# A gated long convolution beside a product-key expert layer on one core: residual taken from the normalized tokens by matrix products, stored tiles read back plainly, norm sums on ScalarE, wider table rows, and shifted priorities in the planner

## The chip, the cores and the metric

The kernel runs on one core of one Trainium2 chip. The metric is device time in microseconds (us) of one execution. Engines are called as the profile calls them: PE (matrix products; PEld is its weight load), DVE (VectorE), ACT (ScalarE), POOL (GpSimd, which here issues the gathers) and SP (the queue that issues all other transfers). All arithmetic is float32.

## The reference

2048 tokens of width 448 are normalized, and three things are added: the tokens themselves, a gated long convolution, and a product-key expert layer.

```python
xn = _layernorm(x, axis=-1)                 # x = A_q, 2048 x 448
return x + _A_ref(xn, ...) + _B_ref(xn, ...)

# _A_ref: four-tap causal filter on k, times v, then a causal convolution of length 2048 per channel
kv = k_shift * v
y = irfft(rfft(kv padded) * rfft(ssm_k padded))[:S] + kv * ssm_D
return q * y                                # q = xn

# _B_ref: 16 heads, two score rows of 64 keys each; the best 2 of each, the best 2 of the 4 sums
s1 = einsum("nhd,ed->nhe", q1, k1); s2 = einsum("nhd,ed->nhe", q2, k2)
g = softmax(top_s)                          # top_e: which 2 of 4096 experts, per head
act = gelu(einsum("nd,nhkd->nhk", xf, u[top_e]))
out = einsum("nhk,nhk,nhkd->nd", g, act, v[top_e])
```

Each token thus needs 32 rows of u and 32 rows of v. The kernel keeps u and v side by side in one table `uv`, 3584 bytes a row, and gathers 65,536 of them, 235 MB.

## The kernel before

**Tiles.** The tokens form 16 tiles T of 128. For the experts a tile is 8 batches, 128 batches in all (b = 8T + j). A batch is four gathers of 128 rows each (L536), which put one (token, expert) pair on each of 128 partitions, four times. The ring holds 5 batches, and at most 6 gathers are on their way.

**A batch** (`batch`, L560): DVE multiplies the gathered u rows with the tokens (L569, one instruction over 1792 elements); the tokens stand in PSUM, repeated by `spread` (L557), once for a tile. ACT sums each of the four products (L575) and applies gelu (L577). POOL, and DVE from batch 104 on (`LATE`), forms the coefficients (L583, L582). PE multiplies them with the v rows into the accumulator `pv` (L588). After the eighth batch `fold` (L599) ends the tile and `store` (L611) writes it from the tile `fo` to the output.

**Residual.** `fold` loads the tile of x again into `fo` (L603). For T below `T_OUT0` = 9, PE adds it to `pv` by a product with the identity (L605) and ACT copies `pv` to `fo` (L606); from T = 9 on, DVE adds `pv` to `fo` (L608).

**Scores.** In the beginning 16 blocks of weights are loaded (`weights`, L355), multiplied by the keys (L365), transposed and split into two parts. For each tile `turn` (L404) transposes the normalized tokens, `score` (L419) makes four blocks of 11 products (L427 to L431), DVE finds the best (L436, L443), and `pick` (L449) turns them into indices and weights.

**Convolution.** It is a Fourier transform in matrix products, over two groups of channels: part 0 (112 channels, while the scores still run) and part 1 (336 channels, after them, in the space that the score weights leave). Each part has three stages: in (`conv_in`, L628: L638 to L659), middle (33 frequencies, `spectrum` and `inverse`, L681 and L732, one 64 KB matrix loaded for each, L678) and out (`conv_out`, L777: transposes L789, copies L791, products L796, gates on DVE L807 and L812). The gate multiplies the convolution with the normalized tokens. For early tiles it does so in place in `XA` (L807), and needs nothing else of the normalized tokens afterwards; for later tiles it goes to another tile, `g0t` or `G` (L812).

**How the gated convolution reaches the output.** Tiles 0 to 13 (`T_OUT1` = 14) are stored before part 1 is done; when it is, POOL adds `XA` to the stored output by 14 accumulating transfers (L944). For tiles 9 to 15 ACT first copies `g0t` (and, for 14 and 15, `G`) into `XA` (L932), and tiles 14 and 15 add `XA` to `fo` on DVE (L951) before they are stored.

**Norm.** DVE makes mean and variance of a tile (L322, L323), a Newton iteration gives the inverse root (L326 to L337), ACT normalizes in place (L341). Tile 0 is done first, then 1 to 3, then 4 to 15 together.

**What sets the order.** Everything is handed as an operation to a planner (`Plan`, L92): engine, assumed duration, what it reads and writes, and a key. The planner simulates the engines in time and, whenever one is free, gives it the ready operation with the smallest key; the order that results is the program order on every engine, and nothing is reordered on the chip. The keys are due times, written by hand (`tb`, `due`, `CONV`, L209 to L213). The durations are constants, such as 1.0 us for the four products of a batch (L596) and 2.8 us for a block of scores (L432). Each gather also waits for one PE operation that lies before it in the plan (`LEAD`, L956 to L970).

At the end of the program a flag is read; a second pass for ties would run only if it is set, which it isn't here.

Of the kernel before, what the change touches and what calls it, by code (L numbers as in the profile page):

```python
# [34 lines left out]
T_OUT0, T_OUT1 = 9, 14  # L35


def tables():
# [37 lines left out]
    return cst1.astype(np.float32), cst2.astype(np.float32), fq.reshape(NQ, P, P).astype(np.float32)  # L76
# [7 lines left out]
class Op:  # L84
    __slots__ = ("eng", "dur", "fn", "deps", "users", "key", "acq", "rel", "nb", "start", "end", "name", "left", "avail", "pace", "last")
# [6 lines left out]
class Plan:  # L92
# [123 lines left out]
LEAD = 0.5  # L216
LATE = 104
# [16 lines left out]
def one_pass(ctx, tc, x, wq, kk, uv, kvh, cst1, cst2, fq, out, flag):  # L234
# [20 lines left out]
    nmr = ap.tile([P, NT], F32, name="nmr")  # L255
    nw = ap.tile([P, 64], F32, name="nw")
# [29 lines left out]
    def switch():  # L286
# [4 lines left out]
        x1[1] = view(sp.tile([P, 84 * XW], F32, name="x1b"), 1)  # L291
# [157 lines left out]
    def pick(T, b0, b1, key, two=1):  # L449
# [65 lines left out]
        op("ACT", 0.2 + 0.008 * n, lambda: put(idx, 0), r=["pl"], w=[("idx", t, i) for t in tiles for i in half], key=key, name="idx")  # L515
        op("ACT", 0.2 + 0.008 * n, lambda: put(gat, 1), r=["pl"], w=[("gat", t, i) for t in tiles for i in half], key=key, rel=("bank", s), name="gat")
# [43 lines left out]
    def batch(T, j):  # L560
# [36 lines left out]
    ob = [S1[:, 0:D], S1[:, D:2 * D]]  # L597

    def fold(T):  # L599
        k = tb(NB * T + NB) + 1.0  # L600
        o = fo[:, :]
        last = NB * T + NB - 1
        load(o, x[T], MB * D, ["fo"], k - 12.0, nb=k - 16.0, name="xr")  # L603
        if T < T_OUT0:
            op("PE", 0.85, lambda: nc.tensor.matmul(pv[:, :D], ident, o, start=False, stop=False), r=["fo", "c1", ("pv", 0)], w=[("pv", NB)], key=k - 2.0, name="res")  # L605
            op("ACT", act(D), lambda: last_val(nc.scalar.activation(o, pv[:, :D], AF.Copy).ins, last), r=[("pv", j) for j in range(NB + 1)], w=["fo", "pv"], key=k, name="fold")  # L606
# [57 lines left out]
    fmb = [S1[:, P * i:P * i + P] for i in range(4)]  # L664
# [10 lines left out]
    def matrix(q, k):  # L675
        u = nf[0] % 4
# [346 lines left out]
```

## Time and profile before

| | us |
|---|---|
| three runs | 940.2, 943.68, 949.0 (median 943.68) |
| the profiled execution | 950.11, span 948.3 |
| tile 0 stored (L612 issued) | 142.8 |
| scores of the last tile, part 0 of the convolution done | about 550 |
| middle of part 1 done, its out stage begins (first L789) | 829.6 |
| last gate of part 1 (L812) | 916.7 |
| last gather issued (L536) | 925.5 |
| last tile stored (L612 issued) | 940.2 |

The profiled execution is 0.7% above the median of the runs. A busy PE in such a page is not PE at its peak, since products are pipelined and the clock that PE is granted changes: 0.84 of full speed in the mean. Idle time of an engine is listed in the profile with what ended it; where two rows of PE and PEld name the same releaser and the same number of times, they are the same stop seen twice.

### The profile page before, as it was taken

To read this page: it belongs to the slowest core of one execution; us is meant where nothing else is said; L and a number is where in the kernel's file an instruction comes from. 1 tells how busy PE (TensorE), PEld (TensorE's weight loads), DVE (VectorE), ACT (ScalarE), POOL (GpSimd) and SP (SyncE) were. 2 spreads that over 40 slices of the span, in tenths; PEclk is the share of its full clock that TensorE was granted. 3 is DMA by queue.
4 is the path that set the end of the run, shared out by engine and by line. 5 is a ranking of instruction groups with operands and counts; after the bars stand their busy time and mean duration, and the time that the engine had idled before them with its cause. 6 is when DMAs were issued, how large, how long until landed. Compare 5 with 4: busy or idle time off the path is not lost.

```text
span 948.3 us, 13985 instructions
## 1 busy us (share of the span) xinstructions
PE 707.8 (75%) x4070; PEld 412.8 (44%) x4070; DVE 679.5 (72%) x1592; ACT 542.9 (57%) x1800; POOL 606.9 (64%) x754
## 2 busy tenths in 40 slices
PE   4777688677868898879888685666677988877671
PEld 2343455444535565546465453443333433344440
DVE  3479786788757887778777856777778999944451
ACT  2346275545554556656473475556577887855551
POOL 0036567688756765665657577787876776665564
PEclk9887779799878998889979778778789999987855
DMA  9998668788978887897779879999999899988898
GB/s 327 327 345 321 189 216 293 250 306 290 320 255 304 301 273 265 289 325 245 246 272 334 291 261 338 365 341 369 345 324 312 295 322 330 325 294 301 290 284 189
DMA packets 72214, 281.46 MB, mean 297 GB/s; under 512 B 10816, under 2 KB 35648, under 8 KB 72128
## 3 DMA queue, kind: packets, MB, share of 16 engines
q0 software_dynamic: 42976, 238.13, 73.5%
q1 hardware_dynamic: 29152, 42.35, 13.2%
q8 instruction: 34, 0.56, 0.2%
q14 instruction: 52, 0.43, 0.1%
HBM read 273.55 MB, written 6.88 MB: 296 GB/s over the span
## 4 chain that ended last, share of the span: by engine, by line
PE 29%; DVE 19%; issue 18%; POOL 12%; DMA 10%; ACT 7%; another core or an unknown queue 3%; SPq 0%; DVEq 0%; POOLq 0%; ACTq 0%
POOL ring L536 9%; DMA ring<-in_uv_dram,idx 8%; PE pv L588 5%; DVE SC L436 5%; DVE ring L569 5%; PE bank L655 4%; ACT ring L575 3%; PE bank L427 2%; PE bank L796 2%; DMA R<-in_wq_dram 2%; PE bank L428 2%; PE bank L429 2%; POOL cc L582 2%; DVE SC L443 2%
## 5 line engine op out<-in xcount | busy, mean ns | idle before, releaser
L536 POOL DMA_INDIRECT ring<-in_uv_dram,idx x512 | 506.9, 990 | 300.2 <-issue 95.4
L575 ACT ACTIVATE ring<-ring 128x448 f32<-128x448 f32 x512 | 288.5, 567 | 85.6 <-DVE ring L569 70.2
L569 DVE TENSOR_TENSOR ring<-ring,xs 128x1792 f32<-128x1792 f32 x128 | 257.4, 2016 | 95.6 <-DMA ring<-in_uv_dram,idx 81.5
L588 PE MATMUL pv<-ring,cc 128*32 128x448 f32 x1024 | 145.4, 650 | 69.8 <-POOL cc L582 34.4
L436 DVE MAX8 SC<-bank 128x8 f32<-128x64 f32 x512 | 118.5, 231 | 47.9 <-PE bank L431 21.7
L655 PE MATMUL bank<-c,S 128*64 128x132 f32 x896 | 77.5, 329 | 30.8 <-ACT ring L575 8.8
L427 PE MATMUL bank<-WR,xh 128*128 128x512 f32 x192 | 89.4, 466 | 10.9 <-DVE xl L416 4.9
L575 ACT ACTIVATION_READ_ACCUMULATOR ring<-ring 128x1 f32 x512 | 97.1, 190 | 0.0
L655 PEld LDWEIGHTS bank<-c,S 128*64 128x64 f32 x896 | 63.7, 165 | 65.3 <-ACT ring L575 24.4
L429 PE MATMUL bank<-WR,xl 128*128 128x512 f32 x192 | 82.7, 431 | 3.1 <-issue 2.5
L428 PE MATMUL bank<-WR,xh 128*128 128x512 f32 x192 | 82.8, 431 | 0.8 <-DVE WR L386 0.8
L588 PEld LDWEIGHTS pv<-ring,cc 128*32 128x32 f32 x1024 | 22.3, 116 | 122.6 <-POOL cc L582 46.0
L703 PE MATMUL bank<-x1b,S 128*128 128x336 f32 x132 | 51.6, 496 | 12.6 <-ACT x1b L767 5.0
L427 PEld LDWEIGHTS bank<-WR,xh 128*128 128x128 f32 x192 | 40.5, 211 | 42.0 <-issue 17.5
L659 ACT ACTIVATE x1b<-bank 128x264 f32<-128x264 f32 x84 | 30.8, 388 | 44.0 <-PE bank L655 32.5
L714 ACT ACTIVATE S<-bank 64x112 f32<-64x112 f32 x132 | 34.0, 257 | 37.1 <-PE bank L699 16.3
L443 DVE FIND_INDEX8 SC<-SC,bank 128x8 uint32<-128x256 f32 x128 | 52.7, 424 | 0.0
L720 DVE TENSOR_TENSOR S<-bank,S 128x224 f32<-128x224 f32 (+1 forms) x66 | 40.5, 618 | 13.8 <-issue 4.0
L582 POOL TENSOR_TENSOR cc<-sm,c 128x128 f32<-128x128 f32 x104 | 48.2, 463 | 3.3
L746 PE MATMUL bank<-S,c 128*128 128x112 f32 x264 | 42.0, 322 | 6.7 <-issue 2.7
L429 PEld LDWEIGHTS bank<-WR,xl 128*128 128x128 f32 x192 | 40.6, 211 | 14.3 <-issue 2.9
L365 PE MATMUL bank<-R 128*64 128x448 f32 x128 | 31.8, 631 | 19.7 <-DMA R<-in_wq_dram 15.6
(130 smaller groups left out, 1020.1 us busy)
## 6 DMA issues: line engine op xcount, KB each, us to landing
R<-in_wq_dram SPq DMA_DIRECT2D x16, 896.0 KB
S<-in_kvh_dram SPq DMA_DIRECT2D x28, 400.0 KB
ring<-in_uv_dram,idx POOLq DMA_INDIRECT x512
S<-in_fq_dram SPq DMA_DIRECT2D x66, 64.0 KB
fo<-in_x_dram SPq DMA_DIRECT2D x16, 224.0 KB
out_dram<-fo SPq DMA_DIRECT2D x16, 224.0 KB
out_dram<-XA POOLq DMA_DIRECT2D x14, 224.0 KB
XA<-in_x_dram SPq DMA_DIRECT2D x2, 1344.0 KB
```

The source lines that it names most:

```text
L427: nc.tensor.matmul(o, xh[:, c, :], wh[:, c, ns], start=(c == 0), stop=False)
L428: nc.tensor.matmul(o, xh[:, c, :], wl[:, c, ns], start=False, stop=False)
L429: nc.tensor.matmul(o, xl[:, c, :], wh[:, c, ns], start=False, stop=False)
L436: nc.vector.max(mx[:, 8 * n + j, :] if safe else m2[:, m, 2 * j:2 * j + 8], bank[s.i][:, 64 * j:64 * j + 64])
L443: nc.vector.max_index(m4i[:, 2 * m + g, :], m2[:, m, 8 * g:8 * g + 8], bank[s.i][:, 256 * g:256 * g + 256])
L536: g = nc.gpsimd.indirect_dma_start(dst, None, uv, bass.IndirectOffsetOnAxis(ap=idx[:, T % 8, r, j:j + 1], axis=0)).ins
L569: op("DVE", dve(m * D), lambda: nc.vector.tensor_mul(U[:, :m, :], U[:, :m, :], xs[:, :m, :D]), r=["xs"], w=u[:m], key=k, name="prod")
L575: op("ACT", 0.575, lambda r=r: nc.scalar.activation(U[:, r, :], U[:, r, :], AF.Copy, accum_out=aw[:, r:r + 1]), w=[u[r], ("aw", b % 4, r)] ...
L582: last_val(ve.tensor_mul(cc[b % 3], co[:, :, None].broadcast_to([P, 4, 32]), rep[:, None, :].broadcast_to([P, 4, 32])).ins, b - 3)
L588: v = nc.tensor.matmul(pv[32 * r:32 * r + 32, :D], cc[b % 3][:, r, :], ring[:, b % RING, r, D:], start=(j == 0), stop=(j == NB - 1), tile_ ...
L655: nc.tensor.matmul(o[64 * i:64 * i + 64, w * j:w * j + w], src, f1[:, i, :], start=True, stop=True, tile_position=(0, 64 * i))
L703: op("PE", 0.95 * n / 448 + 0.05, lambda t=t, sl=sl: nc.tensor.matmul(bank[sl.i][:, :n], fmb[u], x1[p][:, :, q, t, :], start=True, stop=True),
```

## The change

1. **Residual.** x is no longer loaded a second time. From the norm DVE makes dev = (variance + 1e-5) x rstd, the standard deviation (one more instruction in the Newton step). Once for a tile ACT makes `ds`, the identity times dev; PE adds ds times the normalized tile to `pv`, and for tiles from 9 (15) on the identity times `g0t` (`G`), in new functions `more` and `residual`. ACT ends every tile, with the mean as bias. L605, L608, L932 and L951 go.
2. **Stored tiles.** `T_OUT1` is 15. Instead of the accumulating transfers, SP loads the stored tiles 0 to 14 into the space of part 1's data (all columns for T below 9, the 336 of part 1 after), DVE adds `XA`, SP stores them again.
3. **Norm.** Tiles 4 to 15 get their sums from ACT: a copy with a running sum, a scaling, a square with a running sum.
4. **Tables.** The weights' rows are laid out as 7168 bytes for a partition instead of four of 1792; x lies by partitions, so that several tiles are one row; the frequency matrices are loaded in pairs, 34 loads instead of 66, into two buffers instead of four.
5. **Planner.** Operations get a group name, and `RANK` shifts the keys of each group by a line through four numbers over the range of the group's keys. Two orders are made explicit (`after=`): the copies L512 of one place, and the two gates of one chunk.

```diff
-T_OUT0, T_OUT1 = 9, 14
+T_OUT0, T_OUT1 = 9, 15
...
-    return cst1.astype(np.float32), cst2.astype(np.float32), fq.reshape(NQ, P, P).astype(np.float32)
+    turn = [i for ka in range(16) for i in (ka, 32 - ka)] + [16]
+    fq = fq.reshape(NQ, P, P)[turn].transpose(1, 0, 2).reshape(P, NQ * P)
+    return cst1.astype(np.float32), cst2.astype(np.float32), np.ascontiguousarray(fq.astype(np.float32))
...
 LEAD = 0.5
+RANK = {
+    "DMAc1": (25.0, 18.5, 21.0, 40.5), "DMAc2": (-8.5, -20.0, -9.5, -17.5), "DMAfb": (-29.5, 9.0, 67.0, 15.0),
...
+    "SPfb": (59.0, 65.5, 47.5, 62.5), "SPfm@sp0": (-32.0, -5.5, -8.0, -20.0), "SPfm@sp1": (9.0, 49.5, -6.0, 43.0), "SPkk": (4.0, -17.5, 2.0, 2.0),
...
+    "fin@out0": (-90.0, -32.0, -52.5, -95.0), "fin@out1": (-172.5, -183.0, -139.5, -189.5), "flag": (53.5, 83.5, 133.0, 121.0),
...
+    "pt": (-201.0, -329.0, -246.5, -149.0), "pw": (9.0, 9.0, 9.0, 0.0), "px": (2.0, -16.5, -10.5, -18.5), "res": (203.5, 163.5, 229.5, 139.0),
...
+    "res0": (-163.5, -58.5, -62.5, -78.0), "res1": (4.5, 80.5, 92.5, 108.5), "sc": (-60.5, -0.5, -0.5, -0.5), "spread": (53.5, -72.0, -207.0, -4.5),
...
+        ms = [(0.85, ds, slice(0, D), lambda: XA[:, T, :], ["ds", ("x", T)], "res"), (0.32, ident, slice(0, 112), lambda: g0t[:, T - T_OUT0, :], ["c1", ("G", 0)], "res0"),
...
-            op("PE", 0.85, lambda: nc.tensor.matmul(pv[:, :D], ident, o, start=False, stop=False), r=["fo", "c1", ("pv", 0)], w=[("pv", NB)], key=k - 2.0, name="res")
...
+        i = op("SP", 0.08, lambda T=T, c=c, w=w: nc.sync.dma_start(second["x1b"][:, w], out[T][:, c:]), r=["fb"], w=[("fb", T)], key=k, after=(stored[T],), name="SPfb")
...
     def load_x(a, b, key):
-        load(XA[:, a:b, :], x[a:b].rearrange("t p d -> p t d"), MB * D * (b - a), [("x", t) for t in range(a, b)], key, name="x")
-
-    def norm(a, b, key):
+        load(XA[:, a:b, :], x[:, a:b], MB * D * (b - a), [("x", t) for t in range(a, b)], key, name="x")
+
+    def norm(a, b, key, act_=False):
         n = b - a
         sl = slice(a, b)
-        for t in range(a, b):
+        for t in range(a, b if act_ else a):
+            def f(t=t):
+                nc.scalar.activation(fo, XA[:, t, :], AF.Copy, accum_out=nw[:, 54:55])
+                nc.scalar.activation(mv[:, t, 0:1], nw[:, 54:55], AF.Copy, scale=1.0 / D)
+                nc.scalar.activation(fo, XA[:, t, :], AF.Square, bias=mv[:, t, 0:1], scale=-1.0, accum_out=mv[:, t, 1:2])
+            op("ACT", 1.72, f, r=[("x", t)], w=["fo", ("mv", t)], key=key, name="stats")
+        for t in range(b if act_ else a, b):
...
-            nc.vector.tensor_scalar(va, mv[:, sl, 1], 1e-5, None, op0=ALU.add)
+            nc.vector.tensor_scalar(va, mv[:, sl, 1], 1.0 / D if act_ else 1.0, 1e-5, op0=ALU.mult, op1=ALU.add)
...
+            nc.vector.tensor_mul(dev[:, sl], va, rstd[:, sl])
...
-        load(b.rearrange("p h (c d) -> p (h c) d", c=2), wq[h].rearrange("c p d -> p c d"), MB * 1792, [("wq", h % 4)], k, name="wq")
+        load(b.rearrange("p h n -> p (h n)"), wq[h], MB * 1792, [("wq", h % 4)], k, name="wq")
...
-        op("PE", 1.0, val, r=[("cc", b % 3)] + ([("pv", j - 1)] if j else []), w=[("V", b % RING, r) for r in range(4)] + [("pv", j)] + (["pv"] if j == 0 else []), key=k, name="val")
...
+    def more(T):
+        return range(NB, NB + 1 + (T >= T_OUT0) + (T >= T_OUT1))
+
+    def residual(T):
+        k = tb(NB * T + NB) - 1.0
+        op("ACT", 0.3, lambda: nc.scalar.activation(ds, ident, AF.Copy, scale=dev[:, T:T + 1]), r=[("rs", T), "c1"], w=["ds"], key=k - 10.0, name="ds")
+        ms = [(0.85, ds, slice(0, D), lambda: XA[:, T, :], ["ds", ("x", T)], "res"), (0.32, ident, slice(0, 112), lambda: g0t[:, T - T_OUT0, :], ["c1", ("G", 0)], "res0"),
+              (0.66, ident, slice(112, D), lambda: second["G"][:, T - T_OUT1, :], ["c1", ("G", 1)], "res1")]
+        for n, (d, m, c, v, r, name) in zip(more(T), ms):
+            op("PE", d, lambda m=m, c=c, v=v: nc.tensor.matmul(pv[:, c], m, v(), start=False, stop=False), r=r + [("pv", 0)], w=[("pv", n)], key=k, name=name)
 
     def fold(T):
         k = tb(NB * T + NB) + 1.0
         o = fo[:, :]
         last = NB * T + NB - 1
-        load(o, x[T], MB * D, ["fo"], k - 12.0, nb=k - 16.0, name="xr")
-        if T < T_OUT0:
-            op("PE", 0.85, lambda: nc.tensor.matmul(pv[:, :D], ident, o, start=False, stop=False), r=["fo", "c1", ("pv", 0)], w=[("pv", NB)], key=k - 2.0, name="res")
-            op("ACT", act(D), lambda: last_val(nc.scalar.activation(o, pv[:, :D], AF.Copy).ins, last), r=[("pv", j) for j in range(NB + 1)], w=["fo", "pv"], key=k, name="fold")
-        else:
-            op("DVE", dve(D), lambda: last_val(nc.vector.tensor_add(o, o, pv[:, :D]).ins, last), r=[("pv", j) for j in range(NB)], w=["fo", "pv"], key=k, name="fold")
+        op("ACT", act(D), lambda: last_val(nc.scalar.activation(o, pv[:, :D], AF.Identity, bias=mv[:, T, 0:1]).ins, last), r=[("pv", j) for j in [*range(NB), *more(T)]], w=["fo", "pv"], key=k, name="fold")
...
-    def matrix(q, k):
-        u = nf[0] % 4
+    def matrices(ka, k):
+        u = nf[0] % 2
         nf[0] += 1
-        load(fmb[u], fq[q], MB * P, [("fm", u)], k - 6.0, nb=k - 12.0, r=["S1"], name="fm")
-        return u
-
-    def spectrum(p, q, u, k):
+        n = P if ka == 16 else 2 * P
+        load(fmb[u][:, :n], fq[:, 2 * P * ka:2 * P * ka + n], MB * n, [("fm", u)], k - 6.0, nb=k - 12.0, r=["S1"], name="fm")
+        return [(u, 0), (u, 1)]
...
-        op("DVE", dve(CH * n * tc0), lambda: nc.vector.tensor_mul(xv[:, :tc0], fv()[:, :tc0], xv[:, :tc0]), r=reads, w=wk, key=k,
+        ahead = op("DVE", dve(CH * n * tc0), lambda: nc.vector.tensor_mul(xv[:, :tc0], fv()[:, :tc0], xv[:, :tc0]), r=reads, w=wk, key=k,
...
             op("DVE", dve(CH * n * (NT - tc0)), lambda: nc.vector.tensor_mul(gg(), fv()[:, tc0:], xv[:, tc0:]), r=reads + [("x", t) for t in range(tc0, NT)],
-               w=[("G", p)], key=k, rel=("bank", s), name="gateG")
+               w=[("G", p)], key=k, rel=("bank", s), after=(ahead,), name="gateG")
...
             batch(T, j)
+            if j == 0:
+                residual(T)
...
-    norm(4, NT, 75.0)
+    norm(4, NT, 75.0, True)
...
-    def gated(T, g, v, t0, c0, c1_):
-        op("ACT", act(c1_ - c0), lambda: nc.scalar.activation(XA[:, T, c0:c1_], v()[:, T - t0, :], AF.Copy), r=[("G", p) for p in g], w=[("x", T)],
-           key=tb(NB * T + 4), name="gated")
-
     for T in range(T_OUT0, T_OUT1):
         experts(T)
-        gated(T, (0,), lambda: g0t, T_OUT0, 0, 112)
         o, k = fold(T)
         stored[T] = store(T, o, k + 1.0, ["fo"])
     join(s1_mid, [("zt", i) for i in range(4)])
     conv_last("out1", (1,), T_OUT1, lambda: second["G"])
-
+    join([("x1q", 1, i) for i in range(17)] + ["out_in"], ["fb"])
     for T in range(0, T_OUT1):
-        i = op("POOL", 1.8, lambda T=T: nc.gpsimd.dma_start(out[T], XA[:, T, :], accum_op=ALU.add), r=[("x", T)], key=CONV["out1"][1], after=(stored[T],), name="accum")
-        op("DMA", 2 * MB * D / DMA_RATE, None, key=CONV["out1"][1], after=(i,), name="accumD")
+        c = 0 if T < T_OUT0 else 112
+        k = CONV["out1"][1] + T
+        w = slice(D * T, D * T + D - c)
+        i = op("SP", 0.08, lambda T=T, c=c, w=w: nc.sync.dma_start(second["x1b"][:, w], out[T][:, c:]), r=["fb"], w=[("fb", T)], key=k, after=(stored[T],), name="SPfb")
+        pl.writer[("fb", T)] = op("DMA", MB * (D - c) / DMA_RATE, None, key=k, after=(i,), name="DMAfb")
+        op("DVE", dve(D - c), lambda T=T, c=c, w=w: nc.vector.tensor_add(second["x1b"][:, w], second["x1b"][:, w], XA[:, T, c:]), r=[("x", T)], w=[("fb", T)], key=k + 4.0, name="late")
+        i = op("SP", 0.08, lambda T=T, c=c, w=w: nc.sync.dma_start(out[T][:, c:], second["x1b"][:, w]), r=[("fb", T)], key=k + 4.0, name="SPlate")
+        op("DMA", MB * (D - c) / DMA_RATE, None, key=k + 4.0, after=(i,), name="lateD")
     for T in range(T_OUT1, NT):
         experts(T)
-        gated(T, (0,), lambda: g0t, T_OUT0, 0, 112)
-        gated(T, (1,), lambda: second["G"], T_OUT1, 112, D)
         o, k = fold(T)
-        op("DVE", dve(D), lambda T=T, o=o: nc.vector.tensor_add(o, o, XA[:, T, :]), r=[("x", T)], w=["fo"], key=k, name="add")
         store(T, o, k + 1.0, ["fo"])
+
+    ends = {}
+    for o in pl.ops:
+        a, b = ends.get(o.group, (o.key, o.key))
+        ends[o.group] = min(a, o.key), max(b, o.key)
+    for o in pl.ops:
+        if o.group in RANK:
+            (a, b), v = ends[o.group], RANK[o.group]
+            w = (o.key - a) / (b - a) * (len(v) - 1) if b > a else 0.0
+            i = min(len(v) - 2, int(w))
+            o.key = o.key + (v[i] * (1 - (w - i)) + v[i + 1] * (w - i))
 
...
-        "x": a["A_q"].reshape(NT, P, D),
-        "wq": a["B_w_q"].transpose(1, 2, 0).reshape(H, 4, P, D),
+        "x": a["A_q"].reshape(NT, P, D).transpose(1, 0, 2),
+        "wq": a["B_w_q"].transpose(1, 2, 0).reshape(H, 4, P, D).transpose(0, 2, 1, 3).reshape(H, P, 4 * D),
```

In `RANK` stand 96 groups; the rows above are some of them. Operations whose group it doesn't hold keep their keys.

More of the change, by code (lines that the diff above doesn't have):

```diff
@@ L84 @@
 class Op:
-    __slots__ = ("eng", "dur", "fn", "deps", "users", "key", "acq", "rel", "nb", "start", "end", "name", "left", "avail", "pace", "last")
+    __slots__ = ("eng", "dur", "fn", "deps", "users", "key", "acq", "rel", "nb", "start", "end", "name", "left", "avail", "pace", "last", "group")
 class Slot:
@@ L99, in __init__ @@
         self.ops, self.writer, self.readers = [], {}, {}
+        self.stage = ""
         self.free = {}
@@ L108, in op @@
         o.deps, o.users, o.start, o.pace, o.last = set(after), [], None, None, None
+        o.group = name + self.stage
         for k in r:
@@ L255, in one_pass @@
     nmr = ap.tile([P, NT], F32, name="nmr")
+    dev = ap.tile([P, NT], F32, name="dev")
+    ds = ap.tile([P, P], F32, name="ds")
     nw = ap.tile([P, 64], F32, name="nw")
@@ L290, in switch @@
         second["Y"] = sp.tile([P, 2, CH * 84], F32, name="Y")
-        x1[1] = view(sp.tile([P, 84 * XW], F32, name="x1b"), 1)
+        second["x1b"] = sp.tile([P, 84 * XW], F32, name="x1b")
+        x1[1] = view(second["x1b"], 1)
     def view(t, p):
@@ L337, in newton @@
             nc.vector.scalar_tensor_tensor(nmr[:, sl], mv[:, sl, 0], -1.0, rstd[:, sl], op0=ALU.mult, op1=ALU.mult)
-        op("DVE", 3.2, newton, r=[("mv", t) for t in range(a, b)], w=["nw"] + [("rs", t) for t in range(a, b)], key=key, name="newton")
+            nc.vector.tensor_mul(dev[:, sl], va, rstd[:, sl])
+        op("DVE", 3.4, newton, r=[("mv", t) for t in range(a, b)], w=["nw"] + [("rs", t) for t in range(a, b)], key=key, name="newton")
         for t in range(a, b):
@@ L514, in pick @@
         half = range(4) if two > 1 else range(b0, b1)
-        op("ACT", 0.2 + 0.008 * n, lambda: put(idx, 0), r=["pl"], w=[("idx", t, i) for t in tiles for i in half], key=key, name="idx")
-        op("ACT", 0.2 + 0.008 * n, lambda: put(gat, 1), r=["pl"], w=[("gat", t, i) for t in tiles for i in half], key=key, rel=("bank", s), name="gat")
+        ahead = op("ACT", 0.2 + 0.008 * n, lambda: put(idx, 0), r=["pl"], w=[("idx", t, i) for t in tiles for i in half], key=key, name="idx")
+        op("ACT", 0.2 + 0.008 * n, lambda: put(gat, 1), r=["pl"], w=[("gat", t, i) for t in tiles for i in half], key=key, rel=("bank", s), after=(ahead,), name="gat")
     landed = []
@@ L663, in one_pass @@
     nf = [0]
-    fmb = [S1[:, P * i:P * i + P] for i in range(4)]
+    fmb = [S1[:, 2 * P * i:2 * P * i + 2 * P] for i in range(2)]
     cnt = [0]
@@ L845, in conv_first @@
     def conv_first(name, parts):
+        pl.stage = "@" + name
         tot, done = sum(PARTS[p][1] for p in parts), 0
@@ L850, in conv_first @@
                 done += BC
+        pl.stage = ""
     def conv_mid(name, parts):
+        pl.stage = "@" + name
         for ka in range(17):
@@ L868, in conv_last @@
                 done += n
+        pl.stage = ""
     def join(keys, new, fn=None):
```

26 lines of the change are left out of this document (21 added, 5 removed), and 15 rows, old and new, of the table RANK.

## The prediction

> **What bounds the kernel.** I read the page first (busy times and queues), then the table by stages, then the gathers in the same stages.
>
> ```profile
> span 948.3 us, 13985 instructions
> PE 707.8 (75%) x4070; PEld 412.8 (44%) x4070; DVE 679.5 (72%) x1592; ACT 542.9 (57%) x1800; POOL 606.9 (64%) x754
> q0 software_dynamic: 42976, 238.13, 73.5%
> q1 hardware_dynamic: 29152, 42.35, 13.2%
> ...
> core 0: us, PE busy (x) PEld busy (x) DVE busy (x) ACT busy (x) POOL busy (x), PEclk, DMA share, GB/s
> 0.00:65.00 65.00, 42.87 (x211) 18.86 (x215) 34.70 (x130) 22.45 (x63) 8.45 (x14) 0.91 0.97 346
> 65.00:130.00 65.00, 46.31 (x231) 27.98 (x230) 49.37 (x170) 33.65 (x106) 35.76 (x44) 0.72 0.76 255
> 130.00:300.00 170.00, 131.32 (x779) 79.41 (x779) 128.49 (x373) 89.83 (x316) 125.27 (x160) 0.89 0.82 276
> 300.00:550.00 250.00, 205.29 (x1099) 138.29 (x1100) 192.67 (x549) 143.18 (x519) 159.41 (x213) 0.86 0.82 282
> 550.00:700.00 150.00, 99.59 (x911) 59.19 (x913) 104.59 (x130) 90.18 (x302) 116.77 (x141) 0.77 0.96 344
> 700.00:830.00 130.00, 109.78 (x442) 47.85 (x435) 119.26 (x162) 107.65 (x316) 91.70 (x111) 0.98 0.92 317
> 830.00:918.00 88.00, 66.38 (x384) 40.63 (x386) 43.61 (x72) 49.41 (x160) 53.57 (x58) 0.73 0.88 295
> 918.00:948.30 30.30, 6.25 (x32) 0.61 (x24) 6.75 (x11) 6.50 (x24) 15.98 (x17) 0.50 0.91 206
> ...
> 65.00:550.00 485.00, 263.03 (x271) 0.85 0.81 276
> 550.00:700.00 150.00, 97.26 (x93) 0.77 0.96 344
> ```
>
> The two queues keep the DMA engines busy for 87% of the span, and no engine comes near that. But the share of DMA differs by stage. In the first 65 us it is 0.97 (weights), from 550 to 700 it is 0.96, later about 0.9. From 65 to 550 it is 0.76 to 0.82, while PE stands at 79%, DVE at 76% and ACT at 55%: there nothing is full, and the time is made of waits of one engine for another, thus of the order. The last two rows show POOL's gathers alone (L536): 271 in 485 us up to 550, one in 1.79 us; 93 in the 150 us after, one in 1.61 us.
>
> **The change part by part.** The sum is made against the profiled execution, 950.1 us (its span and 1.8 around it), 0.7% above the median of 943.68.
>
> ```profile
> R<-in_wq_dram SPq DMA_DIRECT2D x16, 896.0 KB
> ...
> DMA packets 6251, 10.88 MB, mean 340 GB/s; under 512 B 192, under 2 KB 6249, under 8 KB 6249
> q1 hardware_dynamic: 6249, 10.85, 97.1%
> ...
> q1 hardware_dynamic: 1806, 3.48, 52.6%
> q0 software_dynamic: 636, 3.66, 50.5%
> ```
>
> *Wide rows of the weights.* The second and third row are 13 to 45 us, weights alone: 0.971 x 16 engines x 32 us over 10.85 MB is 21.8 bytes/ns for an engine. The last two are 44 to 62 us: 23.0 for the short rows, 25.2 for the gathers' long ones. 14.7 MB of weights at 21.8 take 42.1 us on 16 engines, at 25.2 they take 36.4, so the bounds are 0 and -5.7. PE waits for them there, so it counts in full; c2 and x stay beside them: **-4**. The Trainium skill ("DMA: Bandwidth & Descriptors", Specifications) puts the least transfer for line rate at 512 B, and all rows here were at least that; by it this term is 0 and the total 4 us higher. The trace speaks for a little gain, 25.2 against 23.0 side by side.
>
> *Matrices in pairs.* At the 21.8 above, 33 x 2 x 64 KB are 12.4 us of DMA; half as many packets can at most save half, 6 us, in stages where DMA has slack for most of it; at least 0. Near the lower end, since bytes stay: **-1**. Two buffers of pairs hold what four held, so no new wait.
>
> ```profile
> PEld pv L605 <- DMA fo<-in_x_dram: 10.2, 3, 6.2
> SPq L305 <- DMA out_dram<-fo: 27.0, 7, 6.1
> L605 PE MATMUL pv<-fo,c 128*128 128x448 f32 x18 | 10.2, 651 | 8.8 <-DMA fo<-in_x_dram 8.8
> L606 ACT ACTIVATE fo<-pv 128x448 f32<-128x448 f32 x9 | 4.8, 537 | 10.3 <-PE pv L588 6.0 <-PE bank L746 4.1 <-remote 0.2
> L746 PE MATMUL bank<-S,c 128*128 128x112 f32 x264 | 42.0, 322 | 6.7 <-issue 2.7 <-DVE S L720 2.1 <-ACT gat L512 1.9
> L498 ACT ACTIVATE SC<-SC,c 128x128 f32<-128x128 f32 (+2 forms) x48 | 13.6, 355 | 3.5 <-DVE SC L482 2.9 <-issue 0.4 <-ACT WR L382 0.2
> ```
>
> *Residual.* Gone: three stops of PE, 10.2 us in all, for a load that itself waited behind the store (second row, SP); and 16 loads of 224 KB, at 340 GB/s 10.8 us of DMA, of which the seven after 550 (4.7 us) lie where DMA is nearly full. I count 7 and 3, because what ran late behind PE was partly late anyway; bounds 0 and -15. New on PE: for tiles from 9 on 10.2/9 = 1.13 us each, and 2 x 42.0/264 = 0.32 for `g0t`, three times that once for `G`: 7 x 1.45 + 1 = 11 us after 550. They hide, except between 700 and 830 where PE is at 84%, two and a half tiles: +2. ACT's `ds` is 16 x 0.355 = 5.7 us, covered by ACT's 43% idle; without that cover it costs 5.7. Seven ends of tiles move from DVE to ACT: ACT waited 10.3 us before nine of them, 1.1 each, with the next batch's sums queued behind: +2 of 8. Without the load `fo`'s only wait is its last store. Together **-6**, bounds -15 and +8.
>
> ```profile
> L322 DVE BATCH_NORM_STATS2 nw<-XA 128x6 f32<-128x448 f32 x16 | 10.0, 627 | 4.2 <-DMA XA<-in_x_dram 3.8
> L323 DVE BATCH_NORM_AGGREGATE mv<-nw 128x2 f32<-128x6 f32 x16 | 2.9, 182 | 0.6
> L575 ACT ACTIVATE ring<-ring 128x448 f32<-128x448 f32 x512 | 288.5, 567 | 85.6 <-DVE ring L569 70.2
> L575 ACT ACTIVATION_READ_ACCUMULATOR ring<-ring 128x1 f32 x512 | 97.1, 190 | 0.0
> L577 ACT ACTIVATE sm<-sm 128x4 f32<-128x4 f32 x128 | 26.2, 205 | 8.5
> L577 ACT ACT_TABLE_LOAD x1 | 1.3, 1283 | 0.0
> ```
>
> *Norm sums.* DVE loses 12 x (0.627 + 0.182) = 9.7 us between 65 and 130, where it is at 76%. ACT gains 12 x (2 x 0.567 + 2 x 0.190 + 0.205) = 20.6 us, and has 31 us idle there. The ends are -9.7, and +15: two loads of an activation table stand in the trace, one of them the last row, and if the square needed another table than gelu, two for each of 12 tiles would be 31 us more on ACT, half of it ahead of the batches' sums. Only copies, tanh and gelu run there now, so no row excludes it; but the copy, the normalization, tanh and gelu share what is loaded after those two. DVE is the fuller engine: **-4**.
>
> ```profile
> L944 POOL DMA_DIRECT2D out_dram<-XA x14 | 13.1, 1598 | 0.0
> L951 DVE TENSOR_TENSOR fo<-fo,XA 128x448 f32<-128x448 f32 x2 | 1.2, 625 | 0.3 <-issue 0.2
> L812 DVE TENSOR_TENSOR G<-bank,XA x12: 205/206/207, 841.1 to 916.7; 128x56 f32<-128x56 f32 x12
> 830.64 1.39 PE L557 MATMUL xs<-XA,c 32*128 32x448 f32 x8
> 925.52 1.08 POOL L536 DMA_INDIRECT ring<-in_uv_dram,idx  x1 [0.90 <-ACT sm L577]
> 926.52 10.01 POOL L944 DMA_DIRECT2D out_dram<-XA  x11
> 931.85 2.02 DVE L569 TENSOR_TENSOR ring<-ring,xs 128x1792 f32<-128x1792 f32 x1 [6.18 <-DMA ring<-in_uv_dram,idx]
> 940.24 0.34 SPq L612 DMA_DIRECT2D out_dram<-fo  x1
> ```
>
> *Stored tiles.* The last gather was issued at 925.5 and used at 931.85, among accumulating transfers; they also fill the 8 us from the last store to the end. I take 3 of the 6.2 us of that wait and 5 of the 8 from the last store to the end of the span, where the transfers' remainder still runs. In their place: 9 x 224 + 6 x 168 KB = 3.1 MB read and as much written, 9 us of DMA each at 340 GB/s, DVE 15 x about 0.6 = 9 us, 30 issues on SP. They follow the last products of the out stage (loads wait for part 1's space). From 917, loads, adds and stores chained need some 25 us, up to 942: about the 940 of the last tile. Net **-4**; bounds -10, and +20 if the out stage moves back. A new wait: gates in place for tiles below 15 follow tile 14's `spread` (830.64) and its residual; the first gate ran at 841, so this is free while that residual is made early in its tile.
>
> *Order.* The shifted keys change every engine's program. If 65 to 550 went at the 1.61 us a gather of the next stage, 271 x 0.18 = 48 us would go; that is the one end, for DMA would then be full. The other is +10: the planner counts 1.0 us for a batch's products where the trace has 0.96 to 1.72, by the granted clock (0.72 to 0.98 in the stages), so an order tight by its durations can stall. I take **-20**, two fifths of the way to full DMA: it is a fifth of the 102 us that PE, the fullest engine, is idle between 65 and 550 (485 less 46.3 + 131.3 + 205.3), and leaves the stalls of a changing clock in place.
>
> Sum: -4 -1 -6 -4 -4 -20 = -39, 911 us against 950.1; times 943.68/950.1: **905 us**, -4%.
>
> **The rivals.**
> *The order balances all.* -48 in place of -20: 883, at the median 877. For it: DMA at 0.96 for 150 us already. Against it: PE's clock in 65 to 130 is 0.72, and scores and part 0 must be made by then.
> *The order gives nothing.* The other terms stay: 931, at the median 925.
> *The change does not do what it says.* The loads and sums were hidden anyway, the tail is as before: only the weights' -4, 940.
> *Slower: the late residual.* Tile 14's residual is planned near the tile's end (its group's keys are shifted by +139 to +230) and the gates, which hold one of three PSUM banks each, wait for it. Tile 14 ran from 830.64 to 885 or so. With gates from 885 instead of 841, the out stage ends at 917 + 44 = 961 at the old pace, the block follows with 25 us: 986; less the 19 that the other terms give up to there (-4 -1 -6 -4, with a few of order): 967, at the median 960. It decides when the out stage ends after about 935. For it: a dozen gates took 76 us in lockstep with gathers. Against it: the planner sees this dependence, and the keys of the out stage's products are shifted forward.
>
> **How the numbers follow.** 905: 0.35 (own range 890 to 918). 877: 0.14. 925: 0.20. 940, no change: 0.13. 960: 0.18. A measurement of this kernel tells about 1% from no change. So faster 0.69, same 0.13, slower 0.18. The range of 8 in 10 goes from 870 (the first rival with its tail) to 948, and leaves out the slower case and a little below.
>
> **What would show it.** Right: DMA share above 0.85 and a gather in 1.7 us or less from 65 to 550; no PE stop for `fo`; ACT's busy time up by some 30 us, DVE's down by 5; weights' DMA done some 4 us earlier; no POOL transfers at the end, the read-back done within 25 us of the last gate, ahead of the last tile's store. Wrong: a table load beside each square; last gate later than 925; or gathers still at 1.79 us, with waits of PE for DVE or POOL in place of those that went.

## The result, and the profile after

On the chip of the profile the changed kernel takes 909.93 us (median of 4 runs, 906.84 to 912.46) against 942.61 before (4 runs): ratio 0.9642, 95% interval 0.9582 to 0.9702. Times here and below are medians of all runs, ratios compare the means of the fast runs alone, so the two can differ by half a per cent. The profiled execution took 912.46 us, its span is 910.7. The forecast was 905 us, or 911 against the profiled execution of before. First the head of the page after, with rows of its table by stages (length, busy us of each engine, granted clock of PE, DMA share, GB/s) and, below the last "...", the rows of POOL's gathers alone:

```profile
span 910.7 us, 14005 instructions
PE 701.0 (77%) x4100; PEld 409.5 (45%) x4100; DVE 676.3 (74%) x1577; ACT 569.5 (63%) x1874; POOL 590.6 (65%) x740
...
0.00:65.00 65.00, 46.73 (x244) 21.75 (x246) 35.56 (x146) 33.06 (x98) 14.95 (x22) 0.99 0.96 384
130.00:300.00 170.00, 135.76 (x801) 82.70 (x799) 137.26 (x388) 95.66 (x339) 128.16 (x167) 0.90 0.87 297
300.00:550.00 250.00, 201.27 (x1209) 128.34 (x1207) 198.52 (x519) 159.90 (x563) 182.19 (x242) 0.91 0.91 315
550.00:700.00 150.00, 106.23 (x814) 61.70 (x810) 110.93 (x140) 97.16 (x306) 107.94 (x129) 0.83 0.90 316
...
65.00:550.00 485.00, 288.64 (x296) 0.89 0.87 301
550.00:700.00 150.00, 91.98 (x87) 0.83 0.90 316
```

From 65 to 550 us there are now 296 gathers instead of 271: one in 1.64 us instead of 1.79, at a DMA share of 0.87 for 0.81. PE's granted clock is higher too: 0.89 for 0.85 there, and 0.84 for 0.72 from 65 to 130. No run separates what the clock gives from what the order gives. From 550 to 700 there are fewer than before, 87 for 93. The times at which the stores of the tiles are issued (start, duration) show the same from the other side. Tile 7 and tile 9, before and then after:

```profile
532.32 0.34 SPq L612 DMA_DIRECT2D out_dram<-fo  x1
636.86 0.34 SPq L612 DMA_DIRECT2D out_dram<-fo  x1
```

```profile
487.18 0.34 SPq L662 DMA_DIRECT2D out_dram<-fo  x1
582.89 0.34 SPq L662 DMA_DIRECT2D out_dram<-fo  x1
```

Tile 7 is 45 us earlier, tile 9 is 54. The end is only 37.6 us earlier. So part of the gain is given back after 583 us. The rows of the first product of part 1's middle stage (first and last start) show where, before and after:

```profile
L703 PE MATMUL bank<-x1b,S x132: 446/446/897, 695.0 to 817.7; 128*128 128x336 f32 x132
```

```profile
L756 PE MATMUL bank<-x1b,S x132: 446/446/929, 659.0 to 796.8; 128*128 128x336 f32 x132
...
L865 DVE TENSOR_TENSOR G<-bank,XA x12: 175/177/177, 816.7 to 892.9; 128x28 f32<-128x28 f32 x12
```

The middle stage starts 36 us earlier and takes 137.8 us instead of 122.7. DMA stands at 0.92 there after and at 0.93 before (PE's clock at 0.94 and 0.97), but 92 gathers lie in the stage instead of 78: the new order lets the gathers run ahead of the convolution, and the convolution shares that stretch with more of them. Runs 1, 3 and 4 below, all on one chip, fit this: without the shifts the stage took 118.0 us with 73 gathers in it, with them 128.7 us with 92 and 135.5 us with 96. The twelve gates of the out stage take 76.2 us (75.6 before), and the last one starts 23.8 us earlier than the 916.7 of before. Then the end, from the timeline after:

```profile
846.84 20.34 SPq L1003 DMA_DIRECT2D x1b<-out_dram  x15
883.78 0.94 POOL L582 DMA_INDIRECT ring<-in_uv_dram,idx  x1 [1.52 <-ACT S L844]
893.66 7.41 DVE L1005 TENSOR_TENSOR x1b<-x1b,XA 128x336 f32<-128x336 f32 x15
894.19 1.40 SPq L1006 DMA_DIRECT2D out_dram<-x1b  x3
897.40 0.34 SPq L662 DMA_DIRECT2D out_dram<-fo  x1
897.83 7.62 SPq L1006 DMA_DIRECT2D out_dram<-x1b  x12
```

The last gather is issued 9 us ahead of the last gate (before: 8.8 us behind it). The stored tiles were fetched back long before the out stage is done, and after the last gate only adds and stores remain: 17.8 us to the end of the span, where it was 31.6. In sum: -45 us up to tile 7, +21 from there to the last gate, -14 after it.

The groups of the new work (busy us, mean ns of one):

```profile
L652 PE MATMUL pv<-XA,ds 128*128 128x448 f32 x32 | 17.3, 627 | 0.0
L658 ACT ACTIVATE fo<-pv,mv 128x448 f32<-128x448 f32 x16 | 10.1, 629 | 9.9 <-PE pv L634 6.7 <-PE bank L458 1.8 <-issue 1.4
L363 ACT ACTIVATE fo<-XA,mv 128x448 f32<-128x448 f32 x12 | 8.0, 669 | 0.4
L648 ACT ACTIVATE ds<-c,dev 128x128 f32<-128x128 f32 x16 | 6.3, 394 | 2.9 <-PE pv L652 2.9
L623 ACT ACT_TABLE_LOAD x1 | 1.3, 1283 | 0.0
```

The residual's products with `ds` wait for nothing. The squares (L363) bring no table load: there are two in the whole trace, as before, and this is the second.

### The profile page after: what moved, and what is told of

Its sections match the earlier page's. It is cut to its first block, busy times and chain, and to the rows that moved or that the text cites. A ratio compares the mean times of both kernels' runs of the same rounds, so it can differ in the third digit from the quotient of the medians.

```text
span 910.7 us, 14005 instructions
## 1 busy us (share of the span) xinstructions
PE 701.0 (77%) x4100; PEld 409.5 (45%) x4100; DVE 676.3 (74%) x1577; ACT 569.5 (63%) x1874; POOL 590.6 (65%) x740
## 5 line engine op out<-in xcount | busy, mean ns | idle before, releaser
L705 PE MATMUL bank<-c,S 128*64 128x132 f32 x896 | 82.8, 340 | 27.2 <-ACT ring L621 12.9
L473 PE MATMUL bank<-WR,xh 128*128 128x512 f32 x192 | 86.9, 453 | 10.3 <-issue 3.6
L705 PEld LDWEIGHTS bank<-c,S 128*64 128x64 f32 x896 | 66.2, 171 | 62.0 <-ACT ring L621 27.5
L475 PE MATMUL bank<-WR,xl 128*128 128x512 f32 x192 | 78.8, 411 | 0.5 <-DVE xl L462 0.5
L474 PE MATMUL bank<-WR,xh 128*128 128x512 f32 x192 | 78.8, 410 | 0.3 <-DVE WR L432 0.3
L688 DVE TENSOR_TENSOR S<-S 128x1024 f32<-128x1024 f32 x28 | 34.6, 1234 | 24.2 <-PE bank L705 16.2
L849 PE MATMUL bank<-c,S 128*128 128x64 f32 x168 | 33.2, 357 | 12.9 <-ACT S L844 10.5
L849 PEld LDWEIGHTS bank<-c,S 128*128 128x128 f32 x168 | 29.4, 261 | 29.9 <-ACT S L844 18.5
L475 PEld LDWEIGHTS bank<-WR,xl 128*128 128x128 f32 x192 | 38.1, 199 | 10.3 <-DVE xl L462 1.2
```

The source lines that it names most:

```text
L473: nc.tensor.matmul(o, xh[:, c, :], wh[:, c, ns], start=(c == 0), stop=False)
L474: nc.tensor.matmul(o, xh[:, c, :], wl[:, c, ns], start=False, stop=False)
L475: nc.tensor.matmul(o, xl[:, c, :], wh[:, c, ns], start=False, stop=False)
L705: nc.tensor.matmul(o[64 * i:64 * i + 64, w * j:w * j + w], src, f1[:, i, :], start=True, stop=True, tile_position=(0, 64 * i))
L849: nc.tensor.matmul(bank[s.i][:, 64 * j:64 * j + 64], z[:, P * (j - a):P * (j - a) + P], f3, start=True, stop=True)
```

## The experiments

Chips differ: the kernel before took 907.06 us on the chip of the first four runs, 944.59 on that of the next four, 910.5 on that of the last four. So each run is compared with the kernel before, or with another kernel, on its own chip.

**1. No shifts.** All of the change, but the keys as written by hand.

```diff
-RANK = {
-    "DMAc1": (25.0, 18.5, 21.0, 40.5), ...
+RANK = {}
```

> The changed kernel with an empty table RANK: parts 1 to 4 of the change, the hand-written keys as before. Theory (the order carries about half, -20 of -33): 925 to 932 us, a gather in 1.72 to 1.77 us between 65 and 550. Rival A (the order carries nearly all): 938 to 950, a gather at 1.79 as before. Rival B (the order carries nothing, the new structure does): 905 to 915.

892.33 us, ratio 0.9788 (0.9707 to 0.987): about what was expected if the order carries half. Against the two runs with shifts on this chip (runs 3 and 4, 874.38 and 878.9 us) the shifts are worth 13 to 18 us by the medians and 9 to 13 by the ratios; the other parts together are worth 15 by the medians and 19 by the ratio. The changed kernel itself was not run on this chip. But the pace of the gathers is not what was expected. POOL's gathers from 65 to 550 us, in this run and then in run 3:

```profile
65.00:550.00 485.00, 294.99 (x304) 0.90 0.88 308
```

```profile
65.00:550.00 485.00, 308.47 (x315) 0.92 0.91 320
```

Without the shifts a gather goes out every 1.60 us, with them every 1.54 (run 4: 307 gathers, 1.58). So the shifts let 1 to 4% more gathers go out, where the whole change gives 9% on the chip of the profile (296 for 271). The kernel before was not traced on this chip, so what the other parts give to the pace isn't shown. What the shifts give is seen in part up to there and in part at the end: tile 7 is stored 11 to 16 us earlier with them, the last gate comes 6 to 10 us earlier, and from it to the end pass 17.4 and 18.3 us instead of 26.0.

**2. Shifts alone.** The kernel before, with the groups and the table of shifts.

```diff
+    for o in pl.ops:
+        if o.group in RANK:
...
+            o.key = o.key + (v[i] * (1 - (w - i)) + v[i + 1] * (w - i))
```

> The kernel before with the groups and the table RANK added, nothing else of the change; groups that do not exist there have no effect. Theory: the shifts were fitted to the changed kernel's operations, so they give back part of their gain here, 915 to 930 us. Rival A (the order carries nearly all and is a property of the keys): 905 to 915. Rival B (the order is worth nothing without the structure): 940 or more.

935.94 us, ratio 1.0302 (1.0245 to 1.0359). It was expected to be faster than the kernel before; only the rival that gives the order no worth without the structure fits. The same numbers that gain time with the changed operations cost 28 us here. One place is seen in the list of waits (us in total, times, longest):

```profile
PE pv L639 <- DMA fo<-in_x_dram: 19.7, 5, 5.6
```

PE stops for the second load of x five times, not three (8.8 us before), and DVE once for 13.5 us. The shifts suit the changed operations and do not help this planner in general.

**3. Weights in short rows.** The changed kernel with the old layout of the weights: rows of 1792 bytes.

```diff
-        load(b.rearrange("p h n -> p (h n)"), wq[h], MB * 1792, [("wq", h % 4)], k, name="wq")
+        load(b.rearrange("p h (c d) -> p (h c) d", c=2), wq[h].rearrange("c p d -> p c d"), MB * 1792, [("wq", h % 4)], k, name="wq")
```

> The changed kernel with the weights' rows of 1792 bytes again, in the same places; the planned order is the same instruction for instruction. Theory (the wide rows are worth 4 us by the prediction): +3 to +6 us, 913 to 916, the last weights' product some 5 to 10 us later. Rival (worth about 10, as the last weights' product moved from 75 to 65): +8 to +12, 918 to 922. By the least transfer of 512 bytes alone: no difference.

874.38 us, ratio 0.9648 (0.9598 to 0.9698). The transfers from 13 to 45 us (the third line is their rate in 40 equal slices) and the last products of the weights, for this kernel and then for the next one, which has the long rows and runs on the same chip:

```profile
DMA packets 5548, 12.43 MB, mean 388 GB/s; under 512 B 234, under 2 KB 5033, under 8 KB 5290
q1 hardware_dynamic: 5545, 12.40, 103.5%
GB/s 379 493 405 430 430 332 466 448 417 430 361 374 381 381 381 374 390 376 381 388 376 381 383 372 390 376 386 376 352 195 405 399 424 424 366 390 379 388 381 381
...
70.06 1.72 PE L411 MATMUL bank<-R 128*64 128x448 f32 x8 [2.58 <-DVE SC L489]
```

```profile
DMA packets 2025, 12.71 MB, mean 397 GB/s; under 512 B 236, under 2 KB 283, under 8 KB 1767
q1 hardware_dynamic: 1938, 12.16, 94.2%
GB/s 455 430 430 430 358 453 435 430 417 399 430 421 412 421 421 430 430 430 412 403 430 421 412 424 394 385 134 108 340 430 414 401 458 394 421 430 421 358 242 421
...
62.73 1.72 PE L411 MATMUL bank<-R 128*64 128x448 f32 x8 [2.13 <-DVE SC L489]
```

The long rows take less of the engines' time for a byte (12.16 MB in 0.942 x 16 x 32 us are 25.2 bytes/ns, against 23.4 for the short ones). The two means, 388 and 397 GB/s, hide the difference in rate: run 4 has a gap (134 and 108 GB/s), and the first slices of run 3 hold the load of x, whose rows are longer. In slices 11 to 25 of 40, about 21 to 33 us, the short rows come at 379 GB/s and the long ones at 420. The weights' products end 7.3 us earlier. At the end nothing of it can be seen, for this run is no slower than the next; but the next has other shifts, so what the rows are worth at the end isn't measured.

**4. Other shifts.** Every number of the shifts moved at random by up to 4.

```diff
-            (a, b), v = ends[o.group], RANK[o.group]
+            (a, b), v = ends[o.group], [x + y for x, y in zip(RANK[o.group], shift[o.group])]
```

> The changed kernel with every number of RANK moved by a random amount between -4 and +4 (the numbers go up to 1648): how much of the order's gain hangs on the exact plan. Theory (the gain lies in the broad shifts): within 8 us of the changed kernel, 902 to 918. Rival (the exact plan carries it, another plan is as good as the hand-written keys): 920 to 935.

878.9 us, ratio 0.9691 (0.9614 to 0.9767). It is 0.5% slower than run 3, which has the exact shifts but the short rows, and faster than run 1. So most of what the shifts give does not hang on their exact numbers. This is one random draw; what it costs against the changed kernel itself isn't measured, since that was not run on this chip.

**5. The changed kernel** on the second chip, for the next three.

> The changed kernel itself, on the same chip as the three kernels that each take one part out of it. Expected ratio to the kernel before: 0.96 to 0.97 again; all other times of this group are read against it.

907.49 us, ratio 0.9604 (0.9571 to 0.9638).

**6. Accumulating transfers** in place of read-back, add and store.

```diff
-        i = op("SP", 0.08, lambda T=T, c=c, w=w: nc.sync.dma_start(second["x1b"][:, w], out[T][:, c:]), ...
+        i = op("POOL", 1.8, lambda T=T, c=c: nc.gpsimd.dma_start(out[T][:, c:], XA[:, T, c:], accum_op=ALU.add), r=[("x", T)], ...
```

> The changed kernel with accumulating transfers on POOL in place of read-back, add and store, still for tiles 0 to 14. Theory (the tail is bound by what follows the last gate, and the adds and stores cost some 18 us from it to the end): the accumulating transfers also start after the last gate, on POOL one per 1 to 1.6 us, 15 of them 20 us: 0 to +6 us. Prediction's step (the read-back is worth 4): +2 to +6. Rival (accumulating is no worse, the read-back only adds DVE work): -3 to 0.

912.99 us, 5.5 more than run 5 (ratio 0.9676, 0.9642 to 0.971). Its last gate and the transfers behind it:

```profile
L865 DVE TENSOR_TENSOR G<-bank,XA x12: 174/176/177, 812.6 to 884.4; 128x28 f32<-128x28 f32 x12
...
884.85 11.67 POOL L1003 DMA_DIRECT2D out_dram<-XA  x13 [7.27 <-DVE G L865]
896.76 0.86 POOL L1003 DMA_DIRECT2D out_dram<-XA  x1 [0.24 <-DMA out_dram<-XA]
```

From the last gate to the end of its span (908.7) pass 24.3 us, in run 5 18.5. The last gate itself is 3 us earlier, so the two profiled spans differ by 2.6 only. The read-back pays where the prediction put it, in the tail. The tail is 14 us shorter than before the change: by estimate some 6 are the read-back's, and some 8 are the shifts', for run 1's tail is that much longer without them.

**7. Norm sums on DVE** again.

```diff
-    norm(4, NT, 75.0, True)
+    norm(4, NT, 75.0)
```

> The changed kernel with the norm sums of tiles 4 to 15 on DVE again (two instructions in place of five on ACT). Prediction's step: +4 us (bounds -15 to +10). Rival (ACT, at 78% between 65 and 130 now, has become the fuller engine there, and the sums are better on DVE): -3 to -6 us.

933.17 us, 25.7 more (ratio 0.9895, 0.9855 to 0.9935), far above the 4 of the prediction's term. Tile 0 is stored 8 us earlier than in run 5, tile 1 4 us later and tile 4 32 us later; after that the loss stays between 21 and 27 us. The stage from 130 to 300, for this kernel and then for run 5:

```profile
130.00:300.00 170.00, 126.38 (x702) 80.65 (x698) 124.31 (x360) 92.98 (x317) 116.19 (x149) 0.82 0.82 273
```

```profile
130.00:300.00 170.00, 134.75 (x806) 83.01 (x806) 138.22 (x391) 96.32 (x342) 129.89 (x168) 0.91 0.89 302
```

All engines do less there, and PE's clock is 0.82 for 0.91. The 9.7 us that DVE gets back don't explain 25.7; run 11 takes this up.

**8. Second load of x** again: x into `fo`, a product with the identity instead of `ds`.

```diff
-        op("ACT", 0.3, lambda: nc.scalar.activation(ds, ident, AF.Copy, scale=dev[:, T:T + 1]), ...
-        ms = [(0.85, ds, slice(0, D), lambda: XA[:, T, :], ["ds", ("x", T)], "res"), ...
+        load(fo[:, :], x[:, T], MB * D, ["fo"], k - 11.0, nb=k - 15.0, name="xr")
+        ms = [(0.85, ident, slice(0, D), lambda: fo[:, :], ["fo", "c1"], "res"), ...
```

> The changed kernel with x loaded a second time into fo and added by PE with the identity (all 16 tiles), instead of ds times the normalized tokens; no ds, no bias. Prediction's step (stops of PE for the load, 10.8 us of DMA): +6 to +10 us, and waits of PE for the load of fo in the trace. Rival (the loads are hidden, PE's stops were late work anyway): -2 to +2.

955.9 us, 48.4 more than run 5, and slower than the kernel before (ratio 1.0117, 1.0069 to 1.0166). Two of its waits:

```profile
PE pv L652 <- DMA fo<-in_x_dram: 31.1, 10, 6.5
POOL ring L582 <- PE pv L652: 27.8, 10, 6.7
```

PE stops ten times for the load, and the gathers, which wait for PE, stop with it. In the kernel before PE stopped three times, for 8.8 us. Like run 7 this says what the part is worth in an order that was made for its absence. The next runs ask what two parts are worth alone.

**9. The changed kernel** on the third chip.

> The changed kernel itself, to stand beside the three others on their chip. Ratio to before 0.957 to 0.968; span from the last gate to the end 17 to 18.5 us.

863.8 us, ratio 0.9508 (0.9473 to 0.9543): better than on the other two chips and than expected. Last gate to end: 17.4 us.

**10. The residual alone.** The kernel before with the products of the residual and of the gated columns, `T_OUT1` left at 14, no shifts, accumulating transfers.

```diff
+            if j == 0:
+                residual(T)
...
-        load(o, x[T], MB * D, ["fo"], k - 12.0, nb=k - 16.0, name="xr")
...
-        gated(T, (0,), lambda: g0t, T_OUT0, 0, 112)
```

> The kernel before with one part of the change: the residual from the normalized tokens on PE (and the gated columns of tiles 9 to 15 by products as well), no second load; hand-written keys, no shifts, accumulating transfers at the end as before. Theory A, the second load stops PE and the gathers by itself: the undoing under the shifts cost 48 us, the stops of PE on that load in the kernel before add up to 10 us, so the part alone gives 10 us or more: ratio below 0.990. Theory B, the load is harmful only together with an order that was searched without it: the part alone gives the 6 us of the prediction's term or less, ratio 0.992 to 1.005.

930.4 us, ratio 1.0232 (1.0196 to 1.0267): slower, which neither theory had. Its trace, the store of tile 10 first:

```profile
637.66 0.34 SPq L627 DMA_DIRECT2D out_dram<-fo  x1
...
L827 DVE TENSOR_TENSOR G<-bank,XA x12: 203/205/206, 793.0 to 866.9; 128x56 f32<-128x56 f32 x12
...
849.10 0.95 POOL L545 DMA_INDIRECT ring<-in_uv_dram,idx  x1 [0.30 <-issue]
867.28 1.93 POOL L957 DMA_DIRECT2D out_dram<-XA  x2 [17.23 <-DVE G L827]
871.13 1.09 POOL L545 DMA_INDIRECT ring<-in_uv_dram,idx  x1 [1.92 <-ACT fo L623]
...
913.01 0.95 POOL L545 DMA_INDIRECT ring<-in_uv_dram,idx  x1 [0.30 <-issue]
...
871.04 4.61 PE L597 MATMUL pv<-ring,cc 128*32 128x448 f32 x24 [0.76 <-ACT fo L623]
...
870.35 0.63 ACT L623 ACTIVATE fo<-pv,mv 128x448 f32<-128x448 f32 x1 [5.58 <-PE pv L597]
925.46 0.63 ACT L623 ACTIVATE fo<-pv,mv 128x448 f32<-128x448 f32 x1 [2.44 <-PE pv L597]
```

The same places in run 11, the kernel before with the norm sums alone:

```profile
648.63 0.34 SPq L621 DMA_DIRECT2D out_dram<-fo  x1
...
L821 DVE TENSOR_TENSOR G<-bank,XA x12: 203/205/207, 794.4 to 872.7; 128x56 f32<-128x56 f32 x12
```

Tile 10 is 11 us earlier than there, the last gate 5.8. (Run 11 is itself 3.3 us faster than the kernel before, of which there is no trace on this chip; against that kernel the last gate would be some 9 us earlier, by estimate.) Then it falls behind. Tile 14 takes the gated columns of part 1 through `pv` now and can't be folded before the last gate (866.9, fold at 870.35). There is one accumulator, so tile 15 can't begin its products (they start at 871.04, after the fold); the ring is full, no gather is issued from 849.10 to 871.13, and POOL's own program stands at an accumulating transfer that waits for the same gate (17.23 us). The other gathers go out between accumulating transfers up to 913. From last gate to end: 64.7 us, against 31.7 in run 11. That is 33 us, and 33 less 5.8 is the whole difference of the two spans (931.6 and 904.4). How much of the 33 is the stop of 22 us and how much the transfers between the late gathers isn't separated. In the kernel before, tiles 14 and 15 got these columns by an add after the fold, and `pv` was free. `T_OUT1` = 15, which the change brings with the stored tiles, leaves one tile of this kind, and its gathers are done when the last gate comes (883.78 and 892.9 above).

**11. The norm sums alone.** The kernel before with the edit of run 7 the other way round.

> The kernel before with another part alone: the sums of the norms of tiles 4 to 15 by ScalarE instead of VectorE, hand-written keys. Theory A, the 25 us of its undoing under the shifts are its own: ratio 0.975 to 0.985. Theory B, the order was fitted to it and it has the size of the prediction's term, 4 us: ratio 0.990 to 1.002. A third way, ScalarE is the later of the two at that place without the shifts: above 1.005.

906.65 us, ratio 0.9964 (0.9935 to 0.9992): 3.3 us (0.7 to 5.9), the size of the prediction's term. So the 25.7 of run 7 are not the price of DVE's work by itself; they come with an order that was made for the other place of it. Why the clock of PE was lower in that order stays open.

**12. Late adds in two parts.** The changed kernel; the late add and store of the columns up to 336 after the 8th gate, of the last 112 after the last one.

```diff
+        u = op("DVE", dve(m), lambda ...: nc.vector.tensor_add(second["x1b"][:, D * T:D * T + m], ..., XA[:, T, c:CUT]),
+               key=k + 4.0, after=(gates[CHUNK - 1], pl.writer[("fb", T)]), name="early")
```

> The changed kernel with the late adds and stores cut in two by columns: those up to column 336 after the 8th of the 12 gates of the last convolution, the last 112 columns after the last gate in two adds and two transfers. Theory: the last 17.7 us, from the last gate to the end, are 7.4 us of adds and 11 us of stores that wait for the last gate though most of their columns are ready 20 to 30 us earlier, while the DMA engines stand nearly idle (share 0.00 to 0.35 from 885 to 895); the tail falls to 8 to 11 us and the ratio to before by 0.007 to 0.010 against the changed kernel on the same chip, the time to about 8 us less. Rival: the early adds stand in VectorE's queue ahead of gates and sums and push the last gate back by as much: the same time within 3 us.

865.64 us, ratio 0.9518 (0.9483 to 0.9552): as run 9. But the edit missed its mark:

```profile
L867 DVE TENSOR_TENSOR G<-bank,XA x12: 171/176/177, 776.7 to 846.0; 128x28 f32<-128x28 f32 x12
...
802.47 16.11 SPq L1008 DMA_DIRECT2D x1b<-out_dram  x15
...
847.56 4.63 DVE L1011 TENSOR_TENSOR x1b<-x1b,XA 128x224 f32<-128x224 f32 x12
```

The first early add starts after the last gate. The loads were issued from 802 on, but the planner still believed that they follow the last transposes of the out stage, and the adds stand in DVE's program where the plan has them. So nothing was done earlier (20.0 us from the last gate to the end, 17.4 in run 9), and whether the tail can be shortened so stays open.

## Why the prediction was right, and where it wasn't

The likeliest case came about: 909.93 against 905, in its own range of 890 to 918, and in the profiled execution 912.46 against the sum's 911. The terms:

| term | predicted | measured |
|---|---|---|
| wide rows | -4 | 7 us earlier where the weights end; at the end not seen, and not measured alone (run 3 against 4) |
| matrices in pairs | -1 | not tried alone |
| residual | -6 | -5.8 up to the last gate (run 10 against 11), +33 behind it, with `T_OUT1` at 14 |
| norm sums | -4 | -3.3 alone (run 11), -25.7 in the new order (run 7) |
| stored tiles | -4 | -5.5 (run 6 against 5) |
| order | -20 | -13 to -18 by the medians, -9 to -13 by the ratios (run 1 against 3 and 4) |

*Wide rows.* Bytes per ns rose to the bound that was worked out, 25.2, and the rate from 379 to 420 GB/s. By the Trainium skill ("DMA: Bandwidth & Descriptors", Specifications: 512 bytes as the least transfer for line rate) this term was to be 0. The transfers of runs 3 and 4 don't agree with it, for both row lengths lie above 512 bytes; the end of the kernel shows no gain, but no run measures this part alone.

*Residual.* The stops for `fo` are gone, and in the changed kernel the products hide, as predicted. In run 10, where `T_OUT1` stays at 14, "they hide" fails for the products of `G`: they don't cost by their length but by where they stand, in an accumulator that tile 15 needs. The prediction listed `T_OUT1` only in its steps on gates in place and named the mechanism in its slower rival, for tile 14 and the gates, but not that the residual without `T_OUT1` = 15 ends 33 us late, with accumulating transfers. In the whole change this cost doesn't arise, so the sum is not touched by it.

*Stored tiles.* "They follow the last products of the out stage" was wrong: the landing space is only the first part of part 1's data, which is transposed early, and the loads are issued at 846.8, 46 us before the last gate. So not 25 us but 17.8 are left behind the gate; and the late stores end the program, not the last tile's (897.4).

*Norm sums.* No table load came, and the bound of +15 fell away.

*Order.* The size is near the forecast, its place isn't. "Two fifths of the way" was meant for 65 to 550; there the gathers went nearly all of it, from 1.79 to 1.64 us where 1.61 was the end. By run 1 the shifts are only a part of that: 304 gathers without them, 315 and 307 with them on one chip, 1 to 4% more where the whole change gave 9%. Up to tile 7 all terms but that of the stored tiles gave -35 us at most, the trace has -45. Then 21 us are given back up to the last gate, where the prediction had no loss, and the tail gives 14 where it had 4. These three misses, 10 too little, 21 too much and 10 too little, cancel, so that the sum agrees within 2 us is luck. What was not seen is that the end hangs on the last gate of part 1: gathers that run 54 us ahead at tile 9 lie in the middle stage, which takes 15 us longer, and the twelve gates take 76 us as before (69 to 80 in the other runs). What sets the pace of these gates isn't shown. In those 76 us ACT waits 21.3 us for the transposes and DVE 19.5 us for gathers. In run 10 no gather is issued after 849.10, and its last three gates still come 6.3 to 7.6 us apart, as the ones ahead of them (6.7 in the mean); but PE's clock is 0.50 there and 0.72 ahead of it.

Of what would show it, the rest came as said: ACT's busy time up by 27 us, DVE's down by 3, no POOL transfer at the end. The rivals: the order did not balance all, nor give nothing; the slower case needed the out stage to end after 935, and it ended at 893.

## What to carry to other kernels

A part of a change that is undone in an order made for the whole shows what that order would lose, not what the part is worth: 25.7 and 48.4 us here, where alone the one gives 3.3 and the other, up to the last gate, 5.8 against run 11. When an operand is moved into an accumulator, ask which tile behind it needs that accumulator, and when the operand comes at the latest. When one stream is made faster, look for the stream that ends last: what runs ahead of it comes back as a longer stage there.

## What the runs showed of the hardware that was not expected

- Chips differ by 4%: the kernel before took 907 to 945 us, and the ratio of the change moved with the chip too, from 0.9508 to 0.9642. On the chip of runs 5 to 8, where it took 937 to 946 us, PE's granted clock was 0.835 to 0.856; on the two where it took 903 to 914 us it was 0.855 to 0.888.
- From 21 to 33 us, where the weights stream, rows of 1792 bytes came at 379 GB/s and rows of 7168 bytes at 420 (runs 3 and 4, one chip), both with the DMA engines busy throughout.
